# Pre-norm attention and MLP on one core: a fourth maximum in the MLP's bursts, scores of two groups moved into the MLP's end, and the attention output's copy on ScalarE

## Chip, core and metric

The kernel runs on one core of a Trainium2 chip. The core has a matrix engine (TensorE, PE in the profile, with its weight loads as PEld), VectorE (DVE), ScalarE (ACT), GpSimd (POOL) and SyncE (SP), which issues all of this kernel's transfers. Each engine works through its own instructions in order and waits on semaphores for the others. TensorE writes to PSUM, eight banks of 128x512 float32 values; VectorE and ScalarE read them there. The metric is the device time of one execution in microseconds, lower is better. All times here are microseconds unless marked ns.

## The reference, cut to what matters

One transformer block without a mask: B=1, S=2048, D=512, 32 heads of 16, F=1792, all float32.

```python
def _A_ref(x, wqkv, wo):
    qkv = (x @ wqkv).reshape(B, S, 3, H, Dh) ...      # q, k, v: B, H, S, Dh
    scores = jnp.einsum("bhqd,bhkd->bhqk", q, k) * Dh ** -0.5
    p = _softmax(scores, axis=-1)
    o = jnp.einsum("bhqk,bhkd->bhqd", p, v)
    return (o, heads side by side) @ wo
def _B_ref(x, w1, w2):
    return silu(x @ w1) @ w2
h  = x + _A_ref(_layernorm(x), wqkv, wo)
h2 = h + _B_ref(_layernorm(h), w1, w2)
```

The softmax is exact: each query's maximum over all 2048 keys is found before its exponentials are taken.

## The kernel before, in words

*Stages.* First the rows are normalized and turned, and queries, keys and values projected, with each float32 product split in three (`product`: high by high, low by high, high by low). Then comes attention, query block by query block (`NB` = 4 blocks of 512 rows). An *item* is four heads of one block (32 items in all, 8 a block); it has 16 *groups*, one per 128 keys (`KC`), 512 groups in all. When the eight items of a block are done, its output projection runs beside groups of the next block's first item (`output`), and then the block's whole MLP (`finish_block`, `mlp`) stands between two groups, at the three places in `marks`. The last block's MLP ends the kernel (`finish_last`).

*A group* (`scores`, `one_max`, `values`). Four score matmuls, one per head, each into a bank of kind `st` (four banks), each read by ScalarE, which writes the exponentials (`pt`, a ring of 12 tiles). Between them up to four matmuls of *maxima* work: queries by keys the other way round, for an item that comes later, into a bank of kind `sm` (three banks), each read by VectorE's maximum (`tensor_reduce`). Scores and maxima use 64 and 48 rows of the array, and neighbours use different halves of its rows. Then the four value products of the group two before (`LAG` = 2), added up over an item's 16 groups in the one bank of kind `pv`.

*An item's end* (`finish_item`). ScalarE copies the first 256 columns of `pv` to `pvs` and VectorE the other 256; five transfers carry it on, and the next item's first value product needs the bank free.

*Maxima.* Each item needs 64 of them, 2048 in all, done ahead of its scores. `maxima(g)` sets how many a group takes (at most three, or four at the start and in the two groups behind an MLP) from what is left until each due time, less what the MLPs will take (`BESIDE`). An item's 64 are brought together (`finish_max`), transposed by TensorE into an `sm` bank and copied to `mt` (`place_max`, by VectorE once attention has begun), and two transfers put them beside the queries, where the score matmul subtracts them.

*The MLP* (`mlp`). 14 steps of 128 hidden columns. Step f has 12 first products (into a `st` bank for f = 0, into the `pv` bank afterwards), then `gate`: SiLU and a copy to the high part on ScalarE, the low part on VectorE; then the 12 second products of step f-1 (`second`), added up in four `st` banks. `weave` puts bursts of three maxima in: behind first products 4 and 12 and second product 8 (`BESIDE_C[3]`), or at four places in the steps named by `EXTRA`. From step `QUIET[b]` on there are none. Behind the last step ScalarE loads the exponential's table by a dummy activation, the last second products run, and VectorE adds the rows to the residual. The two groups that follow, `g in marks or g - 1 in marks`, have four scores and four maxima each and no values.

All instructions of an engine keep the order of the program (`mm`, `act`, `dve`, `pin`, `dma`). Lines of the profile are mostly those of helpers: L74 every matmul, L77 transposes, L88 ScalarE, L91 VectorE, L81 GpSimd, L213 the maxima, L94 transfers. Work is therefore told apart by its tiles: `ps_s` scores, `ps_m` maxima, `pt` exponentials, `pv` values or first products, `ps_acc` second products, `ps_wo` output projection.

Of the kernel before, what the change touches and what calls it, by code (L numbers as in the profile page):

```python
# [20 lines left out]
P = 128  # L21
# [19 lines left out]
LAG = 2  # L41
# [17 lines left out]
BURST = 3  # L59

EXTRA = (4, 8), (6,), ()

QUIET = FC, FC, FC - 1


@with_exitstack
def attention_mlp_kernel(ctx: ExitStack, tc: tile.TileContext, x, wqkv, wo, w1, w2, out):
# [136 lines left out]

    def maximum(i, kb, qt, a, j):

        if i not in mx:
            mx[i] = small.tile([P, 2, 2, 4, 4], F32, name="mx", bufs=RING + 1)
            left[i] = 64
        ps = bank("ps_m", "sm")  # L210
        mm(ps, qs[i % RING][64 * j:64 * j + 48, a, qt * P:qt * P + P],
           ks[i % RING][64 * j:64 * j + 48, a, kb * 512:kb * 512 + 512], start=True, stop=True)
        pin(nc.vector.tensor_reduce(mx[i][:, j, a, qt, kb:kb + 1], ps, axis=AX.X, op=ALU.max))  # L213
        left[i] -= 1
        return left[i] == 0
# [16 lines left out]
    def place_max(i, ns):  # L232

        ps = bank("ps_n", "sm" if at["attention"] else "st", F16)
        tr(ps[:32, :P], ns.rearrange("p j r a -> p (j r a)"), ident_h)
        mt = small.tile([32, P], F16, name="mt")
        if at["attention"]:
            dve("tensor_copy", mt, ps[:32, :P])
        else:
            act("copy", mt, ps[:32, :P])  # L240
        for j in range(2):
            dst = qs[i % RING][64 * j + 48:64 * j + 50].rearrange("r a n -> r (a n)")
            pin(nc.sync.dma_start(dst.rearrange("r (a b) -> r a b", b=P), mt[16 * j:16 * j + 16, :]))
        placed.add(i)
# [21 lines left out]

    def one_max(half=None):
# [9 lines left out]
        if maximum(*todo[i, half].pop(0)):  # L277
# [12 lines left out]

    with ExitStack() as pa:
# [52 lines left out]

        def project_qk(b, n, beside=((), 0), scale=False):
# [4 lines left out]
            weave(product(ps, lambda c: wqk_h[:, c, cols], lambda c: wqk_l[:, c, cols],  # L350
                          lambda c: xth[b][:, c, :], lambda c: xtl[b][:, c, :], DC), *beside)
# [263 lines left out]

    def second(b, acc, f, gh, gl, places):
        w2h, w2l = ws.pop(("w2", f))
# [4 lines left out]
        if f < FC - 1:  # L622
            weave(chain.from_iterable(steps), places)
            return
        for t, step in enumerate(steps):
            run(step)
            n = 4 * b + t
# [4 lines left out]
    def mlp(b):  # L632

        first = bank("ps_w1")
        acc = [bank("ps_acc") for _ in range(3)]
        waiting = None
        for f in range(FC):
            tick()
            places = BESIDE_C[4 if f in EXTRA[b] else 3] if f < QUIET[b] else ((), ())
            if f:  # L640
# [7 lines left out]
            weave(product(ps, lambda c: w1h[:, c, :], lambda c: w1l[:, c, :],  # L648
                          lambda c: hth[:, c, :], lambda c: htl[:, c, :], DC), places[0])
# [38 lines left out]
    def finish_last(pending):  # L688
# [94 lines left out]
        for f in range(FC):  # L783
# [13 lines left out]
            if f > 1:  # L797
                second(b, acc, *waiting.pop(0), ())
        split_weights("w2", FC - 1, "dve")
        while waiting:  # L800
            second(b, acc, *waiting.pop(0), ())

    marks = [KC * (8 * b + 1) for b in range(1, NB)]

    def maxima(g):
# [18 lines left out]
    for g in range(groups):  # L824
# [10 lines left out]
        if i in (8, 16, 24):  # L835
            b, n = i // 8 - 1, c - OUTPUT
# [25 lines left out]
        if i in (8, 16, 24) and c > OUTPUT:  # L862
            output(i // 8 - 1, c - OUTPUT - 1)
# [36 lines left out]
```

## Time and profile before

| | |
|---|---|
| median of 3 runs | 1729.4 us (1729.32 to 1729.89) |
| profiled execution | 1728.78 us, span 1727.0 us |
| PE busy | 1683.9 us (98%) |
| DVE busy | 1460.4 us (85%), of it 1281.1 in 2048 maxima of 682 ns |
| ACT busy | 1247.6 us (72%), of it 1019.6 in 2048 exponentials of 616 ns |
| POOL busy | 233.0 us (13%) |
| mean granted TensorE clock | 0.994 |

The busy shares are averages over stages with different limits. In the page's 40 slices ScalarE is at 9 tenths through attention and at 3 to 6 around each MLP, VectorE at 7 to 9 in both; TensorE is at 9 nearly everywhere, but a matmul's duration there includes its way through the array, and two that use different rows overlap. What limits a stage is read from the spacing of its instructions and from what they wait for. The first three MLPs lie at about 509 to 622, 902 to 1014 and 1294 to 1401 us; the last block's fills the end of the span.

### The profile page before, as it was taken

How to read it: one execution, taken by the hardware profiler on the slowest of the kernel's cores; microseconds unless marked ns; L12 is line 12 of the kernel's file. 1: busy time of each engine (PE TensorE's matmuls, PEld its weight loads, DVE VectorE, ACT ScalarE, POOL GpSimd, SP SyncE). 2: the span in 40 equal slices, each digit the busy share in tenths (PEclk: the TensorE clock that was granted, in tenths of full speed). 3: DMA queues.
4: the chain of work that ended last, by engine and by line, in shares of the span. 5: the costliest groups of instructions: out<-in, count | busy, mean ns of one | idle time of the engine just before them, and what ended most of it. 6: DMA issues, size and time to landing. Idle time of an engine off the chain costs nothing.

```text
span 1727.0 us, 28338 instructions
## 1 busy us (share of the span) xinstructions
PE 1683.9 (98%) x10498; PEld 648.1 (38%) x10498; DVE 1460.4 (85%) x2459; ACT 1247.6 (72%) x2465; POOL 233.0 (13%) x318
## 2 busy tenths in 40 slices
PE   6999999999999999999999999999999999999999
PEld 5656422222245532222245542222235542222377
DVE  6899899999978889999978889999978789997343
ACT  5223599999963269999963359999973369999743
POOL 2113300000032310000033310000023310000000
PEclk9999999999999999999999999999999999999999
DMA  6334311121222111111222211111122211100122
GB/s 186 101 80 152 112 35 37 36 48 38 62 70 77 56 48 31 36 42 44 59 59 79 67 40 32 40 38 44 53 70 80 68 34 45 34 11 20 56 80 80
DMA packets 100570, 102.81 MB, mean 60 GB/s; under 512 B 19028, under 2 KB 77204, under 8 KB 100432
## 3 DMA queue, kind: packets, MB, share of 16 engines
q1 hardware_dynamic: 100432, 101.01, 19.8%
q8 instruction: 82, 1.34, 0.3%
q14 instruction: 56, 0.46, 0.1%
HBM read 77.72 MB, written 17.29 MB: 55 GB/s over the span
## 4 chain that ended last, share of the span: by engine, by line
PE 58%; ACT 35%; DVE 4%; DMA 2%; issue 1%; SPq 0%; ACTq 0%; POOL 0%; POOLq 0%; DVEq 0%
ACT pt L88 33%; PE pv L74 19%; PE ps_acc L74 9%; PE ps_m L74 8%; PE ps_s L74 8%; PE ps_qk L74 5%; PE ps_wo L74 3%; PE ps_w L74 3%; DVE mx L213 2%; PE ps_v L74 2%; PE ps_tr L77 1%; DVE ot L91 1%; DMA va<-in_A_wqkv_dram 1%; DMA ks<-kd 1%; DVE pvs L91 1%
## 5 line engine op out<-in xcount | busy, mean ns | idle before, releaser
L213 DVE TENSOR_REDUCE mx<-ps_m 128x1 f32<-128x512 f32 x2048 | 1281.1, 682 | 108.5 <-PE ps_m L74 80.1
L88 ACT ACTIVATE pt<-ps_s 128x512 f32<-128x512 f32 x2048 | 1019.6, 616 | 41.1 <-PE ps_m L74 37.8
L74 PE MATMUL ps_s<-qs,ks 64*128 64x512 f16 x2048 | 550.6, 382 | 4.3 <-ACT pt L88 1.5
L74 PE MATMUL pv<-pt,va 128*17 128x512 f32 x4096 | 540.4, 601 | 6.3 <-DVE pvs L91 6.2
L74 PE MATMUL ps_m<-ks,qs 48*128 48x512 f16 x2048 | 527.7, 382 | 7.3 <-DVE mx L213 5.7
L74 PEld LDWEIGHTS <-ks 64*128 64x128 f16 x2048 | 153.9, 95 | 568.0 <-issue 458.3
L74 PEld LDWEIGHTS pv<-pt,va 128*17 128x17 f32 x4096 | 68.8, 95 | 233.8 <-issue 213.1
L74 PEld LDWEIGHTS <-qs 48*128 48x128 f16 x2048 | 122.8, 94 | 66.8 <-issue 63.1
L88 ACT CAST w2h<-w 128x512 fp32r<-128x512 f32 x56 | 34.7, 619 | 105.5 <-PE ps_acc L74 105.5
L88 ACT ACTIVATE g<-pv 128x512 f32<-128x512 f32 x39 | 23.3, 597 | 105.2 <-PE pv L74 105.2
L81 POOL TENSOR_SCALAR nm<-nm 128x16 f32<-128x16 f32 x32 | 8.3, 259 | 666.4 <-DVE nm L220 666.4
L74 PE MATMUL ps_acc<-w2h,gh 128*128 128x512 f32 x224 | 92.0, 411 | 0.0
L74 PE MATMUL ps_acc<-w2l,gh 128*128 128x512 f32 x224 | 91.3, 408 | 0.0
L74 PE MATMUL ps_acc<-w2h,gl 128*128 128x512 f32 x224 | 88.9, 397 | 0.0
L91 DVE TENSOR_TENSOR gl<-g,gh 128x512 fp32r<-128x512 f32 x56 | 40.2, 717 | 49.9 <-ACT gh L88 49.9
L81 POOL TENSOR_TENSOR w2l<-w,w2h 128x512 fp32r<-128x512 f32 x42 | 53.6, 1277 | 180.2 <-ACT w2h L88 180.2
L74 PE MATMUL pv<-hth,w1l 128*128 128x512 f32 x156 | 65.9, 423 | 0.0
L81 POOL TENSOR_TENSOR ot<-ot,den 128x512 f32<-128x512 f32 (+1 forms) x16 | 20.4, 1275 | 331.0 <-DMA den<-dr 292.8
L74 PE MATMUL pv<-hth,w1h 128*128 128x512 f32 x156 | 62.4, 400 | 0.0
L74 PE MATMUL pv<-htl,w1h 128*128 128x512 f32 x156 | 61.5, 394 | 0.0
L88 ACT ACTIVATE ks<-ps_qk,qk_s 128x512 f32<-128x512 f32 x24 | 16.5, 689 | 61.8 <-PE ps_qk L74 61.8
L81 POOL TENSOR_TENSOR w1l<-w,w1h 128x512 fp32r<-128x512 f32 x42 | 55.2, 1315 | 22.9 <-ACT w1h L88 22.9
(118 smaller groups left out, 1278.0 us busy)
## 6 DMA issues: line engine op xcount, KB each, us to landing
w<-in_B_w_dram SPq DMA_DIRECT2D x112, 256.0 KB
ks<-kd SPq DMA_DIRECT2D x120, 192.0 KB
qs<-qd SPq DMA_DIRECT2D x128, 48.0 KB
kd<-sh SPq DMA_DIRECT2D x16, 256.0 KB
qd<-sh SPq DMA_DIRECT2D x16, 256.0 KB
hx<-in_A_x_dram SPq DMA_DIRECT2D x16, 256.0 KB
out_dram<-ot SPq DMA_DIRECT2D x16, 256.0 KB
ot<-pvs SPq DMA_DIRECT2D x124, 32.0 KB
```

The source lines that it names most:

```text
L74: tc.keep_in_program_order(nc.tensor.matmul(*a, **k))
L77: tc.keep_in_program_order(nc.tensor.transpose(*a))
L81: tc.keep_in_program_order(getattr(nc.gpsimd, op)(*a, **k))
L88: pin(getattr(nc.scalar, fn)(*a, **k))
L91: pin(getattr(nc.vector, fn)(*a, **k))
L213: pin(nc.vector.tensor_reduce(mx[i][:, j, a, qt, kb:kb + 1], ps, axis=AX.X, op=ALU.max))
```

## The change

Four things are changed.

1. *The restart of attention behind an MLP.* The eight scores and exponentials of the two groups behind each mark are taken into the MLP: three behind the eighth of the second products of step 12 (in the place of a burst of maxima), and three and two amid those of step 13. They use the `sm` banks. The two groups themselves then do nothing, and their eight maxima are gone from there. The dummy activation that loads the exponential's table moves ahead of step 12's second products.
2. *Maxima.* The burst amid a step's second products has four maxima instead of three; the first of them goes into the `pv` bank, which is free between the SiLU of step f and the first products of step f+1. No step has a fourth burst any more (`EXTRA` is empty); in the third MLP bursts end one step earlier (`QUIET`). The groups beside the output projection may take four maxima (`most`), which comes to pass in the second and third block. The last projection ahead of attention gets one burst of four, and attention's first plain group starts with one maximum due.
3. *The output's copy.* `pvs` is copied by ScalarE alone, all 512 columns, but for the last item.
4. *The maxima's copy.* `mt` is always copied by ScalarE.

The counts of matmuls, exponentials and maxima stay: 2048 maxima, 35 of them in the `pv` bank. Maxima inside the three MLPs: 129, 126 and 114 before, 132, 132 and 116 afterwards.

```diff
-BESIDE = (132, 132, 117)
+FIRSTS = 8, 16, 24
+BESIDE = (132, 132, 106)
-BESIDE_A = (6,), 6
-BESIDE_C = {3: ((4, 12), (8,)), 4: ((4, 10), (4, 10))}
-BURST = 3
-EXTRA = (4, 8), (6,), ()
-QUIET = FC, FC, FC - 1
+BESIDE_A = {6: 6}, {4: 4}
+BESIDE_C = ({4: 3, 12: 3}, {8: 4}), ({4: 3, 10: 3}, {4: 3, 10: 4})
+EXTRA = (), (), ()
+QUIET = FC, FC, FC - 2
...
-    def maximum(i, kb, qt, a, j):
+    def maximum(i, kb, qt, a, j, ps=None):
...
-        ps = bank("ps_m", "sm")
+        if ps is None:
+            ps = bank("ps_m", "sm")
...
-        if at["attention"]:
-            dve("tensor_copy", mt, ps[:32, :P])
-        else:
-            act("copy", mt, ps[:32, :P])
+        act("copy", mt, ps[:32, :P])
...
-    def burst(n):
-        for _ in range(n):
+    def burst(n, *more):
+        for ps in more:
+            one_max(ps=ps)
+        for _ in range(n - len(more)):
             one_max()
-    def weave(steps, places, n=BURST):
+    def weave(steps, inserts):
         for k, _ in enumerate(steps):
-            if k + 1 in places:
-                burst(n)
+            if k + 1 in inserts:
+                inserts[k + 1]()
...
-                project_qk(b, 2 * g + key, BESIDE_A if n < 19 else ((), 0), True)
+                project_qk(b, 2 * g + key, BESIDE_A[n == 19], True)
...
-    def scores(g, k):
+    def scores(g, k, kind="st"):
...
-        ps = bank("ps_s")
+        ps = bank("ps_s", kind)
...
-        act("copy", pvs[:, :256], pv[:, :256])
-        dve("tensor_copy", pvs[:, 256:], pv[:, 256:])
+        if i == ITEMS - 1:
+            act("copy", pvs[:, :256], pv[:, :256])
+            dve("tensor_copy", pvs[:, 256:], pv[:, 256:])
+        else:
+            act("copy", pvs, pv)
...
         for t, step in enumerate(steps):
-            run(step)
+            weave(step, {k - 3 * t: fn for k, fn in inserts.items()})
...
+        ahead = [(g, m ^ (g % 2)) for g in marks[b:b + 1] + [marks[b] + 1] for m in range(4)]
+        def some_scores(n):
+            for _ in range(n):
+                scores(*ahead.pop(0), "sm")
         for f in range(FC):
             tick()
-            places = BESIDE_C[4 if f in EXTRA[b] else 3] if f < QUIET[b] else ((), ())
+            beside_1, beside_2 = BESIDE_C[f in EXTRA[b]] if f < QUIET[b] else ({}, {})
+            beside_1 = {k: (lambda n=n: burst(n)) for k, n in beside_1.items()}
+            beside_2 = {k: (lambda n=n: burst(n, *[pv] * (n == 4))) for k, n in beside_2.items()}
+            if f == FC - 1:
+                beside_2 = {8: lambda: some_scores(3)}
...
             parts = gate(ps)
+            if f == FC - 1:
+                act("activation", small.tile([P, 1], F32, name="sw"), ident[:, :1], AF.Exp)
             if waiting:
-                second(b, acc, *waiting, places[1])
+                second(b, acc, *waiting, beside_2)
             waiting = f, *parts
-        act("activation", small.tile([P, 1], F32, name="sw"), ident[:, :1], AF.Exp)
-        second(b, acc, *waiting, ())
+        second(b, acc, *waiting, {2: lambda: some_scores(3), 8: lambda: some_scores(2)})
...
-        if g < LAG + 3 or g in marks or g - 1 in marks:
-            at["due"] = 0
+        if g < LAG + 3:
+            at["due"] = 1
             return 4
-        n = max(0, min(3, int(at["due"]), ready - at["done"]))
+        if g in marks or g - 1 in marks:
+            return 0
+        most = 4 if i in FIRSTS and OUTPUT < c < OUTPUT + 5 else 3
+        n = max(0, min(most, int(at["due"]), ready - at["done"]))
...
-            scores(g, k)
+            if (g, k) not in pts:
+                scores(g, k)
```

More of the change, by code (lines that the diff above doesn't have):

```diff
@@ L265, in next_item, with one_max @@
         return at["item"]
-    def one_max(half=None):
+    def one_max(half=None, ps=None):
         i = next_item()
@@ L276, in one_max @@
         at["done"] += 1
-        if maximum(*todo[i, half].pop(0)):
+        if maximum(*todo[i, half].pop(0), ps):
             soon(WAIT, place_max, i, finish_max(i))
-    def burst(n):
-        for _ in range(n):
+    def burst(n, *more):
+        for ps in more:
+            one_max(ps=ps)
+        for _ in range(n - len(more)):
             one_max()
-    def weave(steps, places, n=BURST):
+    def weave(steps, inserts):
         for k, _ in enumerate(steps):
-            if k + 1 in places:
-                burst(n)
+            if k + 1 in inserts:
+                inserts[k + 1]()
     with ExitStack() as pa:
@@ L343, in measure, with project_qk @@
             pin(nc.scalar.reg_load(qk_f, qk_e[:1, :].bitcast(U32)))
-        def project_qk(b, n, beside=((), 0), scale=False):
+        def project_qk(b, n, beside={}, scale=False):
             g, key = divmod(n, 2)
@@ L350, in project_qk @@
             weave(product(ps, lambda c: wqk_h[:, c, cols], lambda c: wqk_l[:, c, cols],
-                          lambda c: xth[b][:, c, :], lambda c: xtl[b][:, c, :], DC), *beside)
+                          lambda c: xth[b][:, c, :], lambda c: xtl[b][:, c, :], DC),
+                  {k: (lambda n=n: burst(n)) for k, n in beside.items()})
             sh = xp.tile([P, 512], F16, name="sh")
@@ L614, in gate, with second @@
         return gh, gl
-    def second(b, acc, f, gh, gl, places):
+    def second(b, acc, f, gh, gl, inserts={}):
         w2h, w2l = ws.pop(("w2", f))
@@ L622, in second @@
         if f < FC - 1:
-            weave(chain.from_iterable(steps), places)
+            weave(chain.from_iterable(steps), inserts)
             return
         for t, step in enumerate(steps):
-            run(step)
+            weave(step, {k - 3 * t: fn for k, fn in inserts.items()})
             n = 4 * b + t
@@ L648, in mlp @@
             weave(product(ps, lambda c: w1h[:, c, :], lambda c: w1l[:, c, :],
-                          lambda c: hth[:, c, :], lambda c: htl[:, c, :], DC), places[0])
+                          lambda c: hth[:, c, :], lambda c: htl[:, c, :], DC), beside_1)
             parts = gate(ps)
+            if f == FC - 1:
+                act("activation", small.tile([P, 1], F32, name="sw"), ident[:, :1], AF.Exp)
             if waiting:
-                second(b, acc, *waiting, places[1])
+                second(b, acc, *waiting, beside_2)
             waiting = f, *parts
-        act("activation", small.tile([P, 1], F32, name="sw"), ident[:, :1], AF.Exp)
-        second(b, acc, *waiting, ())
+        second(b, acc, *waiting, {2: lambda: some_scores(3), 8: lambda: some_scores(2)})
     found = {}
@@ L797, in finish_last @@
             if f > 1:
-                second(b, acc, *waiting.pop(0), ())
+                second(b, acc, *waiting.pop(0))
         split_weights("w2", FC - 1, "dve")
         while waiting:
-            second(b, acc, *waiting.pop(0), ())
+            second(b, acc, *waiting.pop(0))
     marks = [KC * (8 * b + 1) for b in range(1, NB)]
@@ L858, in attention_mlp_kernel @@
             k = m ^ (g % 2)
-            scores(g, k)
+            if (g, k) not in pts:
+                scores(g, k)
             if m < n:
                 one_max(1 - HEADS[k][1])
-        if i in (8, 16, 24) and c > OUTPUT:
+        if i in FIRSTS and c > OUTPUT:
             output(i // 8 - 1, c - OUTPUT - 1)
```

2 lines of the change are left out of this document (1 added, 1 removed).

## The prediction

> **What bounds the kernel now.** I read the page first, then busy time by stage, then the timeline where stages meet. From the page, the span, TensorE's row and the shares of the chain that ended last:
>
> ```profile
> span 1727.0 us, 28338 instructions
> PE 1683.9 (98%) x10498; PEld 648.1 (38%) x10498; DVE 1460.4 (85%) x2459; ACT 1247.6 (72%) x2465; POOL 233.0 (13%) x318
> PE 58%; ACT 35%; DVE 4%; DMA 2%; issue 1%; SPq 0%; ACTq 0%; POOL 0%; POOLq 0%; DVEq 0%
> ```
>
> The chain alternates between TensorE and ScalarE, so the average says little. Stages (columns: stretch, its length, busy us of PE, PEld, DVE, ACT, POOL, granted clock, DMA share, GB/s): attention, an MLP, and the three stretches in which attention starts again behind an MLP.
>
> ```profile
> 660.00:862.00 202.00, 200.20 (x1506) 44.27 (x1503) 190.88 (x323) 199.44 (x408) 7.20 (x18) 1.00 0.15 44
> 893.00:1015.00 122.00, 120.51 (x537) 67.42 (x535) 100.40 (x165) 42.00 (x73) 37.26 (x35) 1.00 0.19 58
> 622.40:633.90 11.50, 10.79 (x49) 2.00 (x48) 9.08 (x17) 8.48 (x16) 0.67 (x3) 0.70 0.26 94
> 1013.90:1025.90 12.00, 11.29 (x50) 2.22 (x51) 9.66 (x18) 8.39 (x16) 0.67 (x3) 0.72 0.21 76
> 1401.30:1409.90 8.60, 7.92 (x48) 1.69 (x49) 8.38 (x15) 7.79 (x16) 0.00 (x0) 1.00 0.32 116
> ```
>
> In attention TensorE and ScalarE are both full and VectorE has 5% left. In the MLP TensorE alone is full; ScalarE sits idle for two thirds. The restart is the loose place, and two of three restarts ran at a reduced clock. The timeline of attention, one plain group and the end of an item:
>
> ```profile
> 702.26 0.39 PE L74 MATMUL ps_s<-qs,ks 64*128 64x512 f16 x1
> 704.22 0.39 PE L74 MATMUL ps_s<-qs,ks 64*128 64x512 f16 x1
> ...
> 693.18 1.09 ACT L88 ACTIVATE pt<-ps_s 128x512 f32<-128x512 f32 x2
> 693.74 0.39 PE L74 MATMUL ps_s<-qs,ks 64*128 64x512 f16 x1
> 694.13 0.40 ACT L88 COPY pvs<-pv 128x256 f32<-128x256 f32 x1
> 694.38 4.14 ACT L88 ACTIVATE pt<-ps_s 128x512 f32<-128x512 f32 x8
> 694.57 0.43 DVE L91 COPY pvs<-pv 128x256 f32<-128x256 f32 x1 [0.44 <-ACT pvs L88]
> 695.05 1.05 PE L74 MATMUL pv<-pt,va 128*17 128x512 f32 x8 [0.26 <-DVE pvs L91]
> 696.84 0.37 PE L74 MATMUL ps_m<-ks,qs 48*128 48x512 f16 x1
> 698.34 0.39 PE L74 MATMUL ps_s<-qs,ks 64*128 64x512 f16 x1
> ```
>
> A group of four scores, three maxima and four value products takes 704.22-702.26 = 1.96 us. ScalarE starts one exponential each 0.48 (693.18 x2, then the copy at 694.13: 0.95/2), so four fill 1.91 and leave it 0.05 a group. The two groups from 693.74 to 698.34 take 4.60 instead of 3.92: an item's end costs 0.68, about half for the values that wait for the second half copy and half for a maximum held up because VectorE was copying.
>
> **The change, part by part.** (1) The restart. Last MLP product and first score of the fourth group behind it, for the three blocks:
>
> ```profile
> 622.12 0.39 PE L74 MATMUL ps_acc<-w2l,gh 128*128 128x512 f32 x1
> 633.89 0.39 PE L74 MATMUL ps_s<-qs,ks 64*128 64x512 f16 x1
> 1013.56 0.39 PE L74 MATMUL ps_acc<-w2l,gh 128*128 128x512 f32 x1
> 1025.87 0.39 PE L74 MATMUL ps_s<-qs,ks 64*128 64x512 f16 x1
> 1401.04 0.39 PE L74 MATMUL ps_acc<-w2l,gh 128*128 128x512 f32 x1
> 1409.86 0.39 PE L74 MATMUL ps_s<-qs,ks 64*128 64x512 f16 x1
> ```
>
> From the end of the product (0.23 behind its start) these are 11.5, 12.1 and 8.6 us for four groups, the first two without values, but with eight maxima that VectorE must read. Afterwards the two groups' eight scores and exponentials already lie inside the MLP, and two ordinary groups follow: 3.92, plus 0.5 that I allow for the transpose of the next maxima and for VectorE's four residual additions that end after the last product. Gain 7.1+7.7+4.2 = 19.0. The full clock is assumed.
>
> (2) What goes into the MLP for it. A step of the MLP:
>
> ```profile
> 610.26 0.60 PE L74 MATMUL ps_m<-ks,qs 48*128 48x512 f16 x3
> 610.69 1.88 DVE L213 TENSOR_REDUCE mx<-ps_m 128x1 f32<-128x512 f32 x3
> 611.82 0.40 PE L74 MATMUL pv<-hth,w1h 128*128 128x512 f32 x1
> 612.52 0.39 PE L74 MATMUL pv<-hth,w1h 128*128 128x512 f32 x1
> 612.84 0.60 PE L74 MATMUL ps_m<-ks,qs 48*128 48x512 f16 x3
> 613.37 0.50 PE L74 MATMUL pv<-hth,w1l 128*128 128x512 f32 x1
> 618.04 0.60 PE L74 MATMUL ps_m<-ks,qs 48*128 48x512 f16 x3
> 534.71 0.60 ACT L88 ACTIVATE g<-pv 128x512 f32<-128x512 f32 x1 [2.56 <-PE pv L74]
> 543.22 0.60 ACT L88 ACTIVATE g<-pv 128x512 f32<-128x512 f32 x1 [3.30 <-PE pv L74]
> ```
>
> Products follow each other at 0.23 (611.82 to 612.52 is three); over a burst of three it is 0.85, so a burst costs 0.62. Three last 0.60 where a single one lasts 0.37 (696.84): the second, of the other half of the rows, runs beside the first, and the third starts 0.22 behind them. So three take two slots. Bursts of 3, 3 and 2 scores: 0.62+0.62+0.41. In blocks 0 and 1 the first stands where a burst of maxima stood, in block 2 all three are new: 1.0+1.0+1.65 = 3.7 lost. ScalarE, idle for 2.6 us before each activation here, takes the eight exponentials; the exponential's table is loaded ahead of them.
>
> (3) Bursts that go. The three steps with a fourth burst take 8.51 (534.71 to 543.22) where an ordinary one takes 7.78 (610.26 to 618.04), and each spreads over two such intervals: 6 x 0.73 = 4.4. Block 2 loses the three bursts of its step 12: 1.9. Gain 6.3.
>
> (4) The fourth maximum. On TensorE it shares a slot with its neighbour, so 0 (0.22 each, 7.7 in all, if two of the same half met). VectorE reads it first: from 610.69, 0.60 apart and 0.68 long (1.88 for three), the four end at 611.38, 611.97, 612.57 and 613.17. The first product into that bank starts at 611.82, so the bank itself holds up nothing, by 0.44. But the next burst's third matmul, due at 612.84+0.22 = 613.06, takes the bank read until 613.17, plus some 0.05 for the semaphore: 0.16 late. 34 steps have such a burst behind them: 5.4 lost. Ends: 0, and a whole reading of 0.60 each, 20; I take the worked-out wait.
>
> (5) The copy on ScalarE alone. Nearest rows for its price and for the next part (the first with busy us and mean ns, the others with shortest, median and longest ns):
>
> ```profile
> L88 ACT COPY va<-ps_v 128x512 f32<-128x512 f32 x16 | 9.2, 587 | 32.6 <-PE ps_v L74 29.5 <-PE ps_tr L77 3.1
> L91 DVE COPY mt<-ps_n x29: 149/202/213, 239.2 to 1588.6; 32x128 f16<-32x128 f16 x29
> L88 ACT COPY mt<-ps_n x3: 250/250/250, 112.6 to 193.5; 32x128 f16<-32x128 f16 x3
> ```
>
> It would run from 694.13 to 694.72, and the values start at 694.78 instead of 695.05: 0.27 won. VectorE copies nothing, so the maximum at 696.84 isn't late: 0.35 won. Against this ScalarE's next four exponentials start 0.23 later (0.48 instead of 0.25), the fourth ends near 696.70, and the next group's fourth score, due near 696.4 by the plain group's spacing, waits for its bank: 0.3 lost. The five DMA issues behind the copy on SP leave 0.27 sooner, and nothing on the path waits for them. Net 0.3 for each of the 28 items that end inside attention: 8.4. Ends: the wait doesn't come (0.6 each, 17), or ScalarE's extra time is paid in full and nothing won (-0.23 each, -6).
>
> (6) The transposed maxima's copy, 0.20 on VectorE, becomes 0.25 on ScalarE. VectorE's held the third maximum's bank until it was done; ScalarE has it done some 0.1 sooner, and its lag is made up at 0.05 a group. Some 20 in attention: I take +1, ends -5 and +3. The two DMAs that carry it into the queries stand behind it on SP as before, three groups or more ahead of the scores that read them. In the MLP ScalarE has idle time for it.
>
> (7) Groups beside the output projection get a fourth maximum, in blocks 1 and 2 (VectorE and TensorE, two of the four):
>
> ```profile
> 485.47 1.85 DVE L213 TENSOR_REDUCE mx<-ps_m 128x1 f32<-128x512 f32 x3
> 485.81 0.50 PE L74 MATMUL ps_wo<-wo_h,oh 128*128 128x512 f32 x1
> 490.86 0.50 PE L74 MATMUL ps_wo<-wo_h,oh 128*128 128x512 f32 x1
> 490.95 1.88 DVE L213 TENSOR_REDUCE mx<-ps_m 128x1 f32<-128x512 f32 x3
> ```
>
> There are three banks, so the fourth matmul waits until the first is read, and VectorE comes to that only behind the row additions and statistics: 490.95+0.68 = 491.63, then 0.05 for the semaphore and 0.31 from a burst's last matmul to the next product (613.06 to 613.37), which moves from 490.86 to 491.99: 1.13 lost. By the other pair 0.7; the fourth group lies between (0.9), and the first still waits for other things (0). 2 x 2.7 = 5.4 lost, ends 0 and 9. (8) One more burst in the last projection: 0.6 lost. The eight maxima that leave each restart fit where groups have room; a plain group takes its 1.96 with or without them.
>
> Sum: 19.0-3.7+6.3-5.4+8.4+1.0-5.4-0.6 = 19.6. The profiled execution took 1728.8 (span 1727.0), so 1709.2; the median of the runs is 0.6 above it: 1710.
>
> **The rivals.** *A, the half clock stays.* In the two restarts at 0.70 and 0.72 TensorE was hardly idle. The third at full clock took 8.6, the others 2.9 and 3.5 more; if the drop comes behind the MLP all the same, 6.4 of (1) is gone: 1716. For it: nothing quoted shows what triggers it; against: the third restart, and no stretch of plain attention or MLP shows it. The Trainium skill, "TensorE: Matmul & The Clock Gate", section "HAM oscillation", ties the half clock to TensorE gaps of over some 3.4 us; these traces have it with TensorE busy for 10.79 of 11.50 us, so by that rule the restart would not be the cause, and this rival is what would follow.
>
> *B, the borrowed bank holds up the first product.* If the product waited for all four readings, it would start at 613.2 instead of 611.82, 1.4 later; 34 times is 48, less the 5.4 of (4): 1753, slower. For it: there is one such bank, and TensorE works in order. Against: the reading that counts comes first in VectorE's order and ends 0.44 early. It decides from (19.6+5.4)/34 = 0.73 a step.
>
> *C, ScalarE becomes the bound.* If 31 copies cost 0.23 more and 20 small ones 0.25, unhidden, and the 9.4 of (5) and (6) fail: 1710+9.4+12 = 1731, no change. For it: 199.4 of 202 us busy; against: 0.05 spare in each of 16 groups an item is 0.8, over the 0.48 added.
>
> *D, the early scores don't do what they are for*: if the exponentials still run only after the last product, 24 x 0.48 = 11.5 comes back: 1721.
>
> **How the numbers follow.** My forecast has 0.70, A 0.12, B 0.05, C 0.07, D 0.06. Faster by over 0.2% (3.5 us, about what a measurement of this kernel can tell from no change) are the forecast, A and D: 0.87, a point off for mixtures; C is the same, 0.06; B and a C that turns out dearer, 0.07. The range: below, the copy at its best end (8.4 more), 1701; above, D's 1721. The forecast's own range is 1703 to 1717 (a part of (5) either way; (4) or (7) at double).
>
> **What would show it.** (1) scores and exponentials before the last MLP product, values within 1.3 us behind it, granted clock 1.00 there; (2) MLP steps of 7.9 with TensorE's waits for maxima; (5) no copy of the output on VectorE, an item's end costing 0.3 to 0.4; (7) a wait of some 1 us for a maximum ahead of the projections in blocks 1 and 2. Wrong it would be with products waiting for maxima in the MLP's bank, ScalarE without idle time in attention, or a low clock in some new place.

## The result, and the profile after

| | median us | ratio to before, 95% interval | profiled execution (span) |
|---|---|---|---|
| before | 1729.4 (1729.25 to 1729.89) | | 1728.78 (1727.0) |
| changed | 1715.3 (1714.97 to 1715.97) | 0.992 (0.990 to 0.994) | 1715.59 (1713.8) |

The change makes the kernel 14.0 us faster where 19.4 had been forecast. From the page of the changed kernel, the engines' row and the shares of the chain that ended last:

```profile
PE 1672.5 (98%) x10498; PEld 647.6 (38%) x10498; DVE 1449.2 (85%) x2399; ACT 1254.9 (73%) x2494; POOL 233.2 (14%) x318
PE 56%; ACT 37%; DVE 4%; issue 2%; DMA 1%; POOL 0%; SPq 0%; ACTq 0%; POOLq 0%; DVEq 0%
```

These rows hardly differ from those of before, so the comparison has to go by stage. Busy time by stretch of the changed kernel (columns as in the prediction): attention, an MLP, and the ends of the three restarts.

```profile
661.00:863.00 202.00, 201.29 (x1520) 44.83 (x1515) 191.40 (x316) 201.00 (x413) 8.46 (x19) 1.00 0.16 46
890.50:1002.50 112.00, 110.74 (x494) 62.08 (x493) 95.37 (x157) 38.13 (x68) 36.83 (x37) 1.00 0.20 57
622.64:626.90 4.26, 4.26 (x34) 0.98 (x33) 4.25 (x8) 4.00 (x10) 0.00 (x0) 1.00 0.48 177
1012.50:1016.50 4.00, 4.00 (x32) 0.91 (x34) 3.87 (x7) 4.00 (x9) 0.00 (x0) 1.00 0.19 52
1396.00:1400.00 4.00, 4.00 (x31) 0.88 (x30) 3.84 (x8) 4.00 (x10) 0.21 (x1) 1.00 0.01 4
```

In attention ScalarE is now busy for 201.0 of 202 us (199.4 before): a copy that VectorE half did is now its own. The restarts are full on TensorE, nearly full on ScalarE and VectorE, and run at the full clock. The timeline of the first restart:

```profile
617.48 1.58 ACT L89 ACTIVATE pt<-ps_s 128x512 f32<-128x512 f32 x3 [0.15 <-PE ps_s L75]
619.60 1.58 ACT L89 ACTIVATE pt<-ps_s 128x512 f32<-128x512 f32 x3 [0.54 <-PE ps_s L75]
621.72 1.09 ACT L89 ACTIVATE pt<-ps_s 128x512 f32<-128x512 f32 x2 [0.54 <-PE ps_s L75]
622.41 0.40 PE L75 MATMUL ps_acc<-w2l,gh 128*128 128x512 f32 x1
623.89 1.05 PE L75 MATMUL pv<-pt,va 128*17 128x512 f32 x8
626.89 0.39 PE L75 MATMUL ps_s<-qs,ks 64*128 64x512 f16 x1
```

The eight exponentials (from 617.48 to 622.81) run amid the last second products. From the end of the last product (622.41 + 0.23 = 622.64) the values follow after 1.25 us, and the next two groups take 4.25 us, to 626.89: 4.4 had been forecast, 11.5 had been the time before.

The time, laid out along the same five stretches of both traces. The last column is the changed kernel profiled once more on another chip, beside the last experiments. A stretch ends where an item's output copy or an MLP's last second product starts; a plus is time won.

| stretch | terms | forecast | profiled | second profile |
|---|---|---|---|---|
| start to the first item's end | (8) | -0.6 | -2.3 | -0.2 |
| the three MLPs | (2) (3) (4) | -2.8 | -3.3 | -3.6 |
| the three restarts | (1) | +19.0 | +19.4 | +19.4 |
| the rest of attention | (5) (6) (7) | +4.0 | -0.7 | +1.1 |
| behind the last item's copy | | 0 | 0.0 | 0.0 |
| sum | | 19.6 | 13.2 | 16.7 |

The large term came as worked out. The miss lies in attention (4.7 us by the first profile, 2.9 by the second) and, in the first profile, in the start. The three rows below are the first matmuls of maxima in the traces of before, of the changed kernel, and of its second profile, one view each:

```profile
44.89 0.61 PE L74 MATMUL ps_m<-ks,qs 48*128 48x512 f16 x4
```

```profile
45.94 0.61 PE L75 MATMUL ps_m<-ks,qs 48*128 48x512 f16 x4
```

```profile
44.13 0.61 PE L75 MATMUL ps_m<-ks,qs 48*128 48x512 f16 x4
```

The last two belong to the same kernel and differ by 1.8 us. So 1.05 us of the start's 2.3 is within what executions vary by ahead of the change; 0.7 are added up to the first exponential and 0.5 in the first item's groups. In the second profile the maxima begin 0.76 early, and the start loses 1.0 behind them.

The item's end, changed kernel (TensorE and ScalarE, from the timeline):

```profile
686.49 0.39 PE L75 MATMUL ps_s<-qs,ks 64*128 64x512 f16 x1
686.88 0.65 ACT L89 COPY pvs<-pv 128x512 f32<-128x512 f32 x1
687.58 1.05 PE L75 MATMUL pv<-pt,va 128*17 128x512 f32 x8
688.56 0.39 PE L75 MATMUL ps_s<-qs,ks 64*128 64x512 f16 x1
689.55 0.37 PE L75 MATMUL ps_s<-qs,ks 64*128 64x512 f16 x1
690.84 0.39 PE L75 MATMUL ps_s<-qs,ks 64*128 64x512 f16 x1
691.51 0.37 PE L75 MATMUL ps_s<-qs,ks 64*128 64x512 f16 x1
```

The copy took 0.65 us (median of the 32 is 648 ns; 617 in the second profile), not the 0.587 of the copy that was used as its price. The two groups from 686.49 to 690.84 take 4.35 where 4.60 were needed before. The values start when the copy ends, 1.09 behind the first score (1.31 before). In the plain group from 690.84 the fourth score comes 0.67 behind the first; in the group from 688.56 it comes 0.99 behind: ScalarE, late by its longer copy, frees the bank 0.3 later, as forecast. Over the 28 items that end inside attention, the two groups of an item's end, first score to first score, exceed plain ones by 12.3 us in sum, where it was 19.8 before (11.6 in the second profile): 7.5 to 8.2 won of 8.4.

Three rows of ScalarE show what limits attention (the first from before, the others around the copy above):

```profile
698.77 27.56 ACT L88 ACTIVATE pt<-ps_s 128x512 f32<-128x512 f32 x56 [0.24 <-PE ps_m L74]
```

```profile
679.57 7.48 ACT L89 ACTIVATE pt<-ps_s 128x512 f32<-128x512 f32 x15
687.34 21.78 ACT L89 ACTIVATE pt<-ps_s 128x512 f32<-128x512 f32 x44
```

The copy ends at 687.53, and the 44 exponentials behind it at 709.12: one ends every 0.49 us. Before it is 0.49, too (27.56 less some 0.6 for the first, over 55). Four take 1.96, a whole plain group. The 0.05 a group that the prediction gives ScalarE to spare came from starts 0.475 apart in a short burst; by the ends there is nothing to spare. VectorE does not set this pace: ten groups of the last item, which have no maxima at all, take 1.96 each in both kernels (from 1604.45 before, from 1591.24 in the changed kernel). By its end the whole copy adds 0.48 to ScalarE's chain (687.05 to 687.53), and an item's end now costs 0.43: the waits are gone, and what is left is close to the copy itself.

An item's maxima are brought together by one more reduction on VectorE and then transposed. The group with the transpose and the one behind it, where they lie away from items' ends and projections, exceed plain ones by 4.1 us in sum before and by 5.9 in both profiles of the changed kernel: a loss of 1.8 where (6) promised 1.0. One such group, from 406.52 to 408.82 (VectorE and TensorE):

```profile
405.81 0.22 DVE L222 TENSOR_REDUCE nm<-mx 128x16 f32<-128x64 f32 x1
405.95 3.07 DVE L215 TENSOR_REDUCE mx<-ps_m 128x1 f32<-128x512 f32 x5
407.28 0.37 PE L75 MATMUL ps_m<-ks,qs 48*128 48x512 f16 x1
408.82 0.39 PE L75 MATMUL ps_s<-qs,ks 64*128 64x512 f16 x1
```

It takes 2.30. Its third maximum starts 0.76 behind the first score (0.45 in the group before it), when the second of VectorE's readings ends: 405.95+0.60+0.68 = 407.23, and 0.05 more. So VectorE is late there ahead of the transpose's copy. Twelve such pairs of groups are over 0.15 longer than plain ones before, 19 in the changed kernel.

A step of the MLP in the changed kernel, from one SiLU to the next:

```profile
534.79 0.60 ACT L89 ACTIVATE g<-pv 128x512 f32<-128x512 f32 x1 [2.71 <-PE pv L75]
537.29 0.39 PE L75 MATMUL pv<-ks,qs 48*128 48x512 f16 x1
537.71 0.69 DVE L215 TENSOR_REDUCE mx<-pv 128x1 f32<-128x512 f32 x1
538.86 0.39 PE L75 MATMUL pv<-hth,w1h 128*128 128x512 f32 x1
539.86 0.76 PE L75 MATMUL ps_m<-ks,qs 48*128 48x512 f16 x3
542.72 0.60 ACT L89 ACTIVATE g<-pv 128x512 f32<-128x512 f32 x1 [2.71 <-PE pv L75]
```

It takes 542.72 - 534.79 = 7.93. The borrowed bank is read from 537.71 to 538.40, and the first product into it starts at 538.86 unhindered: 0.46 to spare (0.44 forecast). The burst at 539.86 lasts 0.76 instead of 0.60, which is the 0.16 of (4). Beside the projection (TensorE: a burst's fourth maximum, twice, and the product behind the second):

```profile
871.54 0.37 PE L75 MATMUL ps_m<-ks,qs 48*128 48x512 f16 x1 [0.40 <-DVE mx L215]
877.72 0.37 PE L75 MATMUL ps_m<-ks,qs 48*128 48x512 f16 x1 [0.85 <-DVE mx L215]
878.02 0.50 PE L75 MATMUL ps_wo<-wo_h,oh 128*128 128x512 f32 x1
```

The fourth matmul waits 0.40 and 0.85 for VectorE, and the projection's product (878.02) stands behind it. Three groups of a block are 0.67, 1.13 and 0.80 longer than before: 2.6 a block, where (7) had 2.7.

### The profile page after: what moved, and what is told of

It reads as the page before. It is cut to its first block, busy times and chain, and to the rows that moved or that the text cites. A ratio compares the mean times of both kernels' runs of the same rounds, so it can differ in the third digit from the quotient of the medians.

```text
span 1713.8 us, 28253 instructions
## 1 busy us (share of the span) xinstructions
PE 1672.5 (98%) x10498; PEld 647.6 (38%) x10498; DVE 1449.2 (85%) x2399; ACT 1254.9 (73%) x2494; POOL 233.2 (14%) x318
## 4 chain that ended last, share of the span: by engine, by line
PE 56%; ACT 37%; DVE 4%; issue 2%; DMA 1%; POOL 0%; SPq 0%; ACTq 0%; POOLq 0%; DVEq 0%
ACT pt L89 36%; PE pv L75 18%; PE ps_acc L75 10%; PE ps_s L75 8%; PE ps_m L75 7%; PE ps_qk L75 5%; PE ps_v L75 3%; PE ps_w L75 3%; DVE mx L215 2%; PE ps_wo L75 2%; PE ps_tr L78 1%; ACT pvs L89 1%; DVE ot L92 0%; DVE st L92 0%; DVE gl L92 0%
## 5 line engine op out<-in xcount | busy, mean ns | idle before, releaser
L215 DVE TENSOR_REDUCE mx<-ps_m 128x1 f32<-128x512 f32 x2013 | 1261.5, 684 | 104.7 <-PE ps_m L75 74.2
L75 PE MATMUL ps_m<-ks,qs 48*128 48x512 f16 x2013 | 516.7, 381 | 7.7 <-DVE mx L215 6.9
```

Source lines behind the costliest of these rows:

```text
L75: tc.keep_in_program_order(nc.tensor.matmul(*a, **k))
```

## The experiments

Theory: the parts of the change add up as in the prediction; the missing microseconds are (5) and (6), which were priced too well, and the start. Rivals: that (4) and (7) are hidden or dearer than worked out; that the half clock, not the place of the exponentials, made the restarts long; that the copy's gain belongs to the rest of the change. The edits are against the changed kernel unless said otherwise. The experiments ran on three other chips, where the kernel before took 1728.9, 1728.9 and 1730.1 us: on one the fourth maximum, the burst and the two copies undone; on another the two without early scores, the borrowed bank and the three edits together; on a third the rest. Compare by ratios. The changed kernel's own is 0.9919 on the chip of its result and 0.9906 (0.9891 to 0.9921) on the third one. No kernel here leaves out work.

**The fourth maximum beside the projection (7).**

```diff
-        most = 4 if i in FIRSTS and OUTPUT < c < OUTPUT + 5 else 3
+        most = 3
```

> The changed kernel with at most three maxima in the groups beside the output projection; the maxima left out there move to plain groups. My theory (the fourth maximum's matmul waits for a bank behind VectorE's row additions and holds up the projection, 0.67+1.13+0.8 = 2.6 us in each of two blocks, seen as 3.76, 4.65, 4.81 beside 3.09, 3.52, 4.02 of extra time in those groups): 5.2 us faster than the changed kernel, 1710.1 us. Rival (that time is hidden elsewhere or comes back where the maxima go): 1715 us.

1708.2 us, ratio 0.9878 (0.9861 to 0.9894): 5 to 7 us less than the changed kernel. The first of the groups above, and the product behind its third maximum:

```profile
868.24 0.38 PE L75 MATMUL ps_m<-ks,qs 48*128 48x512 f16 x1
868.87 0.50 PE L75 MATMUL ps_wo<-wo_h,oh 128*128 128x512 f32 x1
```

No wait stands there, and the three groups have their lengths of before again (3.07, 3.53 and 4.02 over a plain one). The maxima that are no longer taken there fit elsewhere at no visible price, so a fourth maximum in these groups is a plain loss.

**The burst of three behind the borrowed bank (4).** The first burst goes behind the fifth of the first products instead of the fourth, one product (0.23) later.

```diff
-BESIDE_C = ({4: 3, 12: 3}, {8: 4}), ({4: 3, 10: 3}, {4: 3, 10: 4})
+BESIDE_C = ({5: 3, 12: 3}, {8: 4}), ({4: 3, 10: 3}, {4: 3, 10: 4})
```

> The changed kernel with the MLP's first burst behind the fifth instead of the fourth first product. My theory (a step takes 7.91 to 7.93 instead of 7.77 because that burst's third matmul waits 0.16 us for the bank that the burst of four still holds): steps go back to 7.77, 34 x 0.16 = 5.4 us faster than the changed kernel, 1709.9 us. Rival (the step is longer because of the fourth maximum's own slot or VectorE's load, so that the wait only moves to the next burst): 1715 us.

1708.8 us, ratio 0.9882 (0.9865 to 0.9898). The same place of a step (TensorE, borrowed bank and the next burst):

```profile
536.42 0.39 PE L75 MATMUL pv<-ks,qs 48*128 48x512 f16 x1
539.24 0.60 PE L75 MATMUL ps_m<-ks,qs 48*128 48x512 f16 x3
544.17 0.39 PE L75 MATMUL pv<-ks,qs 48*128 48x512 f16 x1
```

The burst lasts 0.60 again and the step 7.75. The three MLPs are 5.1 us shorter in sum. So the fourth maximum is free on TensorE, as worked out, once the next burst doesn't run into VectorE.

**The copy (5), undone.**

```diff
-        if i == ITEMS - 1:
-            act("copy", pvs[:, :256], pv[:, :256])
-            dve("tensor_copy", pvs[:, 256:], pv[:, 256:])
-        else:
-            act("copy", pvs, pv)
+        act("copy", pvs[:, :256], pv[:, :256])
+        dve("tensor_copy", pvs[:, 256:], pv[:, 256:])
```

> The changed kernel with the attention output copied in two halves again, ScalarE and then VectorE. My theory (an item's end costs 0.67 with the halves and 0.43 with one copy, in 28 items, by the two traces): 6.7 us slower than the changed kernel, 1722 us. Rival (ScalarE bounds attention, and its 0.23 longer copy costs as much as the second half's wait): no difference, 1715 us, or faster.

1719.7 us, ratio 0.9942 (0.9926 to 0.9959): 4 to 6 us more than the changed kernel. An item's end shows the two half copies and the wait of before; its sum over 28 items is 17.7 us, 5.4 more than in the changed kernel's first profile.

```profile
688.05 0.41 ACT L89 COPY pvs<-pv 128x256 f32<-128x256 f32 x1
688.49 0.43 DVE L92 COPY pvs<-pv 128x256 f32<-128x256 f32 x1 [0.44 <-ACT pvs L89]
688.97 1.05 PE L75 MATMUL pv<-pt,va 128*17 128x512 f32 x8 [0.26 <-DVE pvs L92]
```

**The copy alone.** The kernel before with this one part of the change.

```diff
-        act("copy", pvs[:, :256], pv[:, :256])
-        dve("tensor_copy", pvs[:, 256:], pv[:, 256:])
+        if i == ITEMS - 1:
+            act("copy", pvs[:, :256], pv[:, :256])
+            dve("tensor_copy", pvs[:, 256:], pv[:, 256:])
+        else:
+            act("copy", pvs, pv)
```

> The kernel before with nothing changed but the output's copy, whole on ScalarE. Theory: the item's end falls from 0.67 to about 0.42 us, and the next group's fourth score is late by the same 0.26 as in the changed kernel: 0.24 x 28 = 6.7 us less, 1722, ratio 0.996. Rival: the gain belongs to the changed kernel alone, because here ScalarE's copies meet the scores' bursts behind the MLPs: within 2 us of the kernel before.

1723.8 us, ratio 0.9969 (0.9957 to 0.9981): 5.4 us (3.3 to 7.4). The sum over the 28 items falls from 19.8 to 12.2. So the copy gains without the other parts, too. Here, too, the copy takes 0.62:

```profile
692.50 0.62 ACT L88 COPY pvs<-pv 128x512 f32<-128x512 f32 x1
693.17 1.05 PE L74 MATMUL pv<-pt,va 128*17 128x512 f32 x8
```

In the group from 694.16 the fourth score is again 0.98 behind the first, 0.31 more than in a plain group.

**The transposed maxima's copy (6), undone.**

```diff
-        act("copy", mt, ps[:32, :P])
+        if at["attention"]:
+            dve("tensor_copy", mt, ps[:32, :P])
+        else:
+            act("copy", mt, ps[:32, :P])
```

> The changed kernel with the transposed maxima copied by VectorE once attention has begun. The prediction had 1 us of gain in this part: then 1716.3 us. By the traces the groups with a transpose cost 3.5 us in all before and 4.1 after: then 1714.7 us. A rival in which the ScalarE copy delays the exponentials in full (20 x 0.25): 1710.3 us.

1713.6 us, ratio 0.9909 (0.9892 to 0.9926), inside the changed kernel's own spread; the groups with a transpose exceed plain ones by 6.1 us in sum, against 5.9 in the changed kernel. It doesn't matter which of the two engines makes this copy. With the kernel before and the output's copy alone the sum is 4.0, so it is not that copy either that made these groups dearer. It goes with the new places of the maxima (all profiles that have them show 5.0 or more); which of the moves does it was not tested.

**No early scores (1), maxima as before.** The scores of the two groups go behind the MLP again, with four maxima each.

```diff
-            if f == FC - 1:
-                beside_2 = {8: lambda: some_scores(3)}
...
-        second(b, acc, *waiting, {2: lambda: some_scores(3), 8: lambda: some_scores(2)})
+        second(b, acc, *waiting)
...
         if g in marks or g - 1 in marks:
-            return 0
+            at["due"] = 0
+            return 4
```

> The changed kernel without the early scores: the two groups behind each MLP have their four scores and four maxima again, and a burst of maxima stands in the place of the first scores. By the two traces the restarts would cost 7.25+7.8+4.3 = 19.4 us more, the score bursts in the MLPs 3.7 less, and the groups beside the projection have three maxima here, 5.2 less: 1715.3+10.5 = 1725.8 us. My theory has the half clock back in the restarts (6.4 of these 19.4). Rival (the half clock was chance and doesn't come back): 1719.4 us, clock 1.00 in the restarts.

**No early scores, and no maxima there.** As the last one, but the two groups take no maxima (`return 0` stays), so that VectorE isn't in their way.

> The same without maxima in the two groups behind an MLP (three of twelve or more scores follow each other alone). Tells what the restart waits for and what drops the clock. Theory 1 (VectorE's readings hold TensorE up, and the clock drops for that): clock 1.00, the restart at ScalarE's pace, 16 x 0.48 = 7.7 and some 0.5 to the fourth group, against 4.4 with the early scores: 3 x 3.8 - 3.7 = 7.7 more, some 2 less for the groups beside the projection: 1721 us. Theory 2 (the clock drops because TensorE has little to do, whoever it waits for): half clock in two or three restarts, 3 us each more: 1727 to 1730 us.

With maxima 1721.5 us (ratio 0.9946, 0.9925 to 0.9967), without 1722.0 (0.9953, 0.9937 to 0.9970). The restarts, from the last second product to the next item's copy, by trace:

| | block 0 | block 1 | block 2 |
|---|---|---|---|
| before | 39.6 | 40.1 | 36.8 |
| changed | 32.3 | 32.3 | 32.6 |
| no early scores, four maxima | 39.6 | 37.0 | 38.4 |
| no early scores, no maxima | 38.6 | 37.1 | 37.2 |

Without maxima in the way the restarts are 0.7 shorter on average, although the clock fell more often; with equal stretches of half clock, in block 0, it is 1.0. So the maxima are the smaller part. What makes the restarts long is chiefly that the exponentials start only behind the products, and the granted clock; the clock falls without those maxima as well. For the kernel without the maxima (the windows of the second restart around the drop, and of the first; the granted clock is the third number from the right):

```profile
1013.17:1016.58 3.41, 2.53 (x12) 0.60 (x9) 0.73 (x3) 3.20 (x8) 0.00 (x0) 1.00 0.77 284
1016.58:1019.99 3.41, 3.41 (x15) 0.52 (x16) 1.94 (x3) 2.83 (x6) 0.00 (x0) 0.50 0.09 20
624.04:630.87 6.83, 6.79 (x30) 1.07 (x27) 3.93 (x6) 5.28 (x12) 0.00 (x0) 0.50 0.07 18
```

and its eight value products inside the half-clock stretch, which take 1.91 us where those of the changed kernel's restart took 1.05 (623.89 above):

```profile
1018.05 1.91 PE L75 MATMUL pv<-pt,va 128*17 128x512 f32 x8
```

All three restarts of this kernel have such a stretch, two of three with four maxima, two of three before, all three of the kernel with the copy alone, and none of the 30 restarts in the ten profiles with early scores. The kernel with maxima came out between its two expectations, because the clock fell in two restarts and in one of them for 3.41 us only; the one without has the time of the one theory and the clock of the other. Restarts with no drop take 36.8 (before, block 2) and 37.0 (four maxima, block 1), early scores 32.4: some 4.5 us a restart, 13.5 in all, are due to what left the restart, and the other 6 of the 19.4 to the clock. With the 1.0 above for the maxima, an estimate from one pair of restarts, some 3.5 of the 4.5 are due to the exponentials' place.

**The borrowed bank last (rival B).** The burst's maximum in the `pv` bank comes fourth instead of first.

```diff
-        for ps in more:
-            one_max(ps=ps)
         for _ in range(n - len(more)):
             one_max()
+        for ps in more:
+            one_max(ps=ps)
```

> The changed kernel with the borrowed bank's maximum last in its burst instead of first. If the order of VectorE's readings decides whether the borrowed bank holds up the first products, as the prediction's 0.44 us of margin says, these now wait for the fourth reading, some 1.4 us a step, and the next burst's wait of 0.16 goes: 34 x 1.24 = 42 us more, 1757 us, steps of 9.1. If the margin is not what keeps it free: 1715 us.

1758.8 us, ratio 1.0164 (1.0140 to 1.0189), slower than the kernel before. The first product of two steps (TensorE):

```profile
541.65 0.51 PE L75 MATMUL pv<-hth,w1h 128*128 128x512 f32 x1 [1.24 <-DVE mx L215]
550.90 0.50 PE L75 MATMUL pv<-hth,w1h 128*128 128x512 f32 x1 [1.24 <-DVE mx L215]
```

Each waits 1.24 us for VectorE, and a step takes 9.25. This is what rival B described; the order inside the burst alone decides between a gain of 14 us and a loss of some 29.

**Three edits together.** Three maxima beside the projection, the burst behind the fifth product, and the transposed maxima's copy on VectorE.

> The changed kernel with all three of the earlier edits that gained: at most three maxima beside the projection, the burst behind the fifth first product, the transposed maxima's copy on VectorE. If they add up (6.7, 6.1 and 1.3 below the changed kernel by the ratios to the kernel before): 1701 to 1703 us. If they share a cause: 1706 or more.

1703.9 us, ratio 0.9851 (0.9832 to 0.9871): faster than both kernels, by 25 us against before. That is 0.9 over the 1701 to 1703 expected if the three add up and 2 below the 1706 of a shared cause, and the interval reaches both. The trace decides for the first two: the MLPs are 5.0 shorter in sum than the changed kernel's, and the three groups beside the projection 5.2 in the two blocks. The third brings nothing, as the next runs show.

**The changed kernel again, and the three edits without the transposed maxima's copy.** No edit, and the first two edits alone.

> The changed kernel again, beside the three below, so that their parts are compared on one chip. Theory: the first two experiments' ratios less the terms that their traces showed put it at a ratio of 0.991 to 0.992, 1713 to 1715 us where the kernel before takes 1729. Rival: if its ratio is 0.990 or less, the sums of the experiments do not add up by 3 us.

> Three maxima beside the projection and the first burst behind the fifth first product, with the transposed maxima's copy left on ScalarE. Theory: that copy is worth nothing on either engine, so the time is that of the three edits together, 1703.9 +- 1. Rival: the 1.3 us or so that the copy on VectorE seemed to bring by its ratio are real: 1705.2.

1713.2 us, ratio 0.9906 (0.9891 to 0.9921), and 1705.4 us, ratio 0.9853 (0.9838 to 0.9868). The two-edit kernel's time is nearer its rival's, but the kernel before was 1.2 us slower on that chip, too, and the ratio is that of the three edits: no difference between the engines shows for the transposed maxima's copy. The first expectation holds by its time, and its ratio lies between the two bounds that were named; 2 us between the same kernel's medians on two chips is what a comparison across chips has to allow for. One thing was not expected in the two-edit kernel: a half-clock stretch amid groups beside the projection, where no other profile has one, and where a group took 1.5 us longer:

```profile
863.45:866.86 3.41, 3.28 (x8) 2.60 (x9) 0.00 (x0) 1.54 (x4) 0.93 (x1) 0.50 0.45 143
```

**Fewer maxima at attention's start.** The three edits together, and attention's first five groups with three maxima in place of four.

```diff
         if g < LAG + 3:
-            at["due"] = 1
-            return 4
+            at["due"] = 0
+            return 3
```

> The three edits together, and attention's first five groups with three maxima each in place of four. Theory: these groups are late because VectorE's maxima are behind, as beside the projection: five maxima fewer at 0.60 us are about 3 us, 1701. Rival: they are late because TensorE's clock is halved there whatever VectorE does: the same as with the three edits, 1704, with a half clock near 200 us still in the trace.

1705.4 us, ratio 0.9856 (0.9841 to 0.9872): no gain, so both expectations are half right. Attention's first groups, by windows, with three maxima and (from the three-edit kernel, in the second fence) with four:

```profile
197.80:212.40 14.60, 14.30 (x79) 3.33 (x76) 11.76 (x20) 12.51 (x26) 6.90 (x8) 0.77 0.54 140
```

```profile
196.99:212.00 15.01, 13.67 (x74) 2.48 (x74) 13.65 (x23) 11.83 (x24) 7.07 (x8) 0.89 0.55 136
```

The first five groups' excess over plain ones falls from 4.5 to 2.9 us, although the clock was lower. But the five maxima are missing at the end: the last item's first score waits for its maxima (TensorE, timeline of the kernel with three):

```profile
1570.45 0.60 PE L75 MATMUL ps_s<-qs,ks 64*128 64x512 f16 x4 [2.87 <-DMA qs<-mt]
```

The 1.6 us won are lost there, and more. Where a kernel has no other place left for a piece of work, taking it away from a crowded stretch only moves the wait.

Not tried: the early scores on the kernel before, without the fourth maximum. The maxima that they displace would have no place there.

## Why the prediction was right, and where it was off

*(1)* right, in place and size: 19.4 for 19.0. The full clock that the sum assumed was granted in every restart. The prediction assumed it, with one restart that had kept it as its only support, and some 6 of the 19 us hang on it: that part was in good part luck, though the clock stayed full in all ten profiles with early scores. The experiments divide the gain, as the prediction didn't: about 70% from the exponentials and maxima that left the restart, most of it the exponentials', and 30% from the clock.

*(2), (3) and (4)* together -3.3 for -2.8. (4) is exact (0.16 a step, 5.4; the experiment gave back 5.1). Of the other two, the MLPs of the kernel without early scores are 1.2, 1.2 and 2.2 us shorter than the changed one's, so the scores' bursts cost 4.7 where (2) said 3.7. With the MLPs' sum that leaves some 6.5 for (3), for 6.3.

*(5)* came nearly in full: 7.5 us (8.2 in the second profile, 7.6 with the copy alone) for 8.4. Both mechanisms are there, the value products freed and the fourth score 0.3 late. The price was a little low: the row taken is a 128x512 copy of 0.587 in a stage where ScalarE had idle time, against 0.62 to 0.65 measured between exponentials. What was won on the values is so 0.22 in the item shown, instead of 0.27. The copy's lag is not made up later, since ScalarE has no 0.05 a group.

*(6)* is the term that failed: -1.8 instead of +1.0, and the larger part of attention's miss. The step that failed is that the copy's engine, with ScalarE's 0.05 a group to absorb it, decides what such a group costs. Undoing the copy changes nothing (6.1 and 5.9), and in the group looked at VectorE is late before the copy. The prediction also put the new places of the maxima at nothing, since a plain group takes its 1.96 with or without them; that holds for plain groups, but not for those with a transpose, where more are now long. Why more are is open.

*(7)* right: 5.2 for 5.4, and the experiment shows that it was an avoidable loss. With (5) and (6) it leaves 1.2 us of attention's loss in the first profile, and 0.1 in the second, that no experiment assigns.

*(8)* The first exponential is 1.8 later in the profile, 0.7 of it behind the first maxima, about the 0.6 of the new burst; the first item's groups lose the rest. Behind the first maxima the start loses 1.2 (1.0 in the second profile), twice the term. The other 1.05 is a variation that precedes the change. The prediction had no term for it and could have none; its range did.

Of the rivals, A (the half clock stays) has the nearest time, 1716, for another reason: the clock did not stay half in any restart. B was avoided by the order in the burst, and its mechanism and price were shown. C named the engine that limits attention: what the prediction held against it, 0.05 spare in each group, isn't there. It failed all the same because it let the copy cost 0.23 on top of the old item's end, 0.68, whose waits the copy removes: 0.43 is left. D did not happen.

The time itself, 5 us over the forecast, lies in the forecast's own range. How large the gain is beyond the restarts is known to some 2 or 3 us: two measurements of the changed kernel have medians of 1715.3 and 1713.2 and profiled spans of 1713.8 and 1710.3.

## What to carry to other kernels

A stage in which one engine is idle can take the next stage's work for that engine, if its inputs are ready and a bank is free: the gain here was some 4.5 us a restart, about what the moved exponentials (eight at 0.49) and maxima had cost there, against 1.2 to 2.2 an MLP for the scores' bursts. When a bank is borrowed for a short while, put the borrowed piece first in the reader's queue, and look where the reader's lag falls next; one product's distance decided some 5 us, and the order in the burst some 43. To find what an engine has to spare, measure from end to end over many instructions, not from start to start over two. Price an operation by a row from a place where its engine is as full as it will be, and count a term as nothing if it relies on the last few per cent of an engine.

## What was not expected of the hardware

The granted clock falls to a half in stretches of 3.41 or 6.83 us, in places where TensorE is fed in small pieces, never in a visible long gap: in the 7 us ahead of any of these drops, the one at the kernel's end apart, TensorE was idle for at most 0.61 us at a time. Ahead of the drop at 1016.58 above it was busy for 2.53 of 3.41 us. The rule on long gaps that the prediction quotes doesn't describe this; the Trainium skill, "TensorE: Matmul & The Clock Gate", section "A second HAM failure mode: psum-queue depth-cycling", comes nearer: it says of another kernel that frequent short idle times between groups of matmuls made the clock go back and forth. That agrees with the rows here. It isn't the whole condition: the kernel before has stretches with a lower busy share that keep the full clock, as this window of its last MLP's start and the full clock in the 3.41 us behind it show.

```profile
1643.18:1646.59 3.41, 2.37 (x20) 1.95 (x17) 1.31 (x3) 1.05 (x2) 0.78 (x2) 1.00 0.02 5
```

What sets it off stays open. The cure shown here is indirect: with the exponentials early the restarts keep the full clock in 30 of 30 cases, without that in 2 of 12; which part of the move does it is not shown.
